# From batch 2 on, key scores in 64x32 tiles with a maximum for each half of the keys, their weights turned by DMA; one more MLP chunk by the seven-product form; a narrower iteration

## The chip, the core and the metric

The kernel runs on one core of a Trainium2 chip. The metric is device microseconds of one execution. A core has a matrix engine (TensorE, "PE" in the profile, with weight loads shown apart as "PEld"), three engines for elementwise work (VectorE "DVE", ScalarE "ACT", GpSimd "POOL"), and SyncE ("SP"), which here issues the DMAs. Data lie in on-chip memory as 128 partitions by columns; matrix products land in eight PSUM banks of 128 x 512 float32.

## The reference, cut

q, k and v have the shape (8 batches, 8 heads, 576 positions, 64); q and k are scaled up by 8.

```python
q_lm = q.reshape(B, H, 32, 18, D).mean(axis=3)      # 32 landmarks
k_lm = k.reshape(B, H, 32, 18, D).mean(axis=3)
A, Bm, C = sm(q, k_lm), sm(q_lm, k_lm), sm(q_lm, k)  # sm: softmax of a b^T / 8
Z = Bm^T / (norm1(Bm) * norminf(Bm) + 1e-6)
for _ in range(6):
    Z = 2 * Z - Z @ Bm @ Z
x = A @ Z @ C @ v                                    # then heads side by side: (8, 576, 512)
u = x + real(fft2(x))                                # over positions and columns
un = layernorm(u)
out = u + relu(un @ w_ch1) @ w_ch2                   # 512 -> 2048 -> 512
```

## The kernel before, in words

**Recording.** The methods of `Kernel` don't emit instructions: they record operations in `Order`, each with a phase, a group, a cost and the tiles it reads and writes. `solve` then lists them by these costs, engine by engine, and takes buffers from pools (`SLOTS`, `BANKS`) as it goes; matmuls between `together` and `apart` stay in one piece. Everything is emitted from one line, L1204 in the profile (L1307 after the change), so groups are told apart by the names of tiles. `SEVEN, LATE = 5, 2`.

**Attention, batch by batch** (`attention`, `landmarks`, `mix`). Heads go in two groups g of four. `lm` holds landmark sums; `qbd` is the landmark queries in blocks, with zeros between. In `landmarks`:
- Bm's scores, softmax, `nrm` (Bm and its row sums), the norms `ci`;
- C's scores for each g: four float32 matmuls `qbd` x `kv` into two banks of 288 keys, one maximum `cb` over both, exp, the sum's reciprocal `cr`;
- `Ce` (C, 128 x 576) turned on PE with the identity (four blocks of 128 and one of 64 into `at` banks, copied to `ml` tiles by ACT), and 20 float32 matmuls for C·v. The result, times `cr` and `ci`, goes into columns 32:96 of the tile `RE`, whose columns 0:32 hold E = 1 − Bm·Z in the block form;
- six rounds of `RE[:, 0:32]` x `RE`, 96 columns wide (the last 64), which square E and carry C·v along; then `pst` and `Wx`, which `mix` takes.

`mix` applies A and the transform over positions, `norm` the layer norm, and it turns `un` by DMA, as two fp16 halves (`hl`), into `unT`.

**MLP**, in 18 chunks of 256 tokens, eight steps i of 256 hidden columns each. Every product of float32 matrices is three fp16 products (high x high, high x low, low x high). The first layer is 48 matmuls of 256 columns per step (`hp<-unT,w`). The second layer of chunks 0 to 4 (`chunk`) is 12 matmuls of 512 columns per step (`acc<-w,h`, or `h` in a `sum` tile). From chunk 5 (`SEVEN`) on, `seven` does it with seven products of quarter matrices, 21 matmuls of 256 columns per step, with sums of weight blocks: three per step (`sums_of`) lie in DRAM and are fetched for each step (`big<-sums`), two (`differences_of`) replace the weights in place. For `seven`, DVE, ACT and POOL make seven combinations of h per step (tiles `ws`, `sum`, `h`). MLP work is low in priority and fills PE where attention waits. E in the code stands for either DVE or POOL.

Attention's products all land in the four `at` banks; `seven` holds two of these from its first chunk on.

Of the kernel before, what the change touches and what calls it, by code (L numbers as in the profile page):

```python
# [98 lines left out]
class Pool:  # L99
    def __init__(self, slots, in_order, kept=False):  # L100
        self.slots, self.in_order, self.kept = slots, in_order, kept
        self.free = list(range(len(slots)))
        self.given, self.made = 0, 0
# [64 lines left out]
class Op:  # L168
    __slots__ = ("engine", "calls", "held", "took", "phase", "group", "margin", "seq", "before", "after", "tiles", "claims", "rank", "start", "end", "nbytes", "port", "name", "other")


class Order:
# [21 lines left out]
    def op(self, engine, held, took, writes, reads, call, nbytes=0, port=False):  # L194
        o = self.bundle if engine == "PE" and self.bundle else None
        if o is None:
            o = Op()
            o.engine, o.calls, o.held, o.took, o.seq = engine, [], 0.0, 0.0, len(self.ops)
            o.phase, o.group, o.margin, o.nbytes, o.port = self.phase, self.group, self.margin, nbytes, port
            o.other = {}  # L200
# [33 lines left out]
    def solve(self):  # L234
# [38 lines left out]

        def able(e, o):
# [8 lines left out]
        while events:  # L283
# [13 lines left out]
            best, again = {}, []  # L297
            for e in engines:
                if free[e] <= now + 1e-9 and ready[e]:
                    best[e] = min((x for x in ready[e] if able(e, x[1]) and fits(x[1])), default=None, key=lambda x: x[0])  # L300
# [5 lines left out]
            for e in [e for e in best if e not in again] + again:  # L306
                found = best[e]
                if found is None or found not in ready[e] or not (able(e, found[1]) and fits(found[1])):
                    found = min((x for x in ready[e] if able(e, x[1]) and fits(x[1])), default=None, key=lambda x: x[0])
# [88 lines left out]
class Kernel:  # L398
    def __init__(self, ctx, tc, NB, q, k, v, w1, w2, t1, t1t, t2, diag, mask, out):
# [13 lines left out]
        for n, (cols, count) in SLOTS.items():  # L413
            self.pools[n] = Pool([self.pool.tile([P, cols], F32, name=f"{n}{i}") for i in range(count)], n in IN_ORDER)
        for n, count in BANKS.items():
            n = "hp" if n == "h" else n
            self.pools[n] = Pool([self.ps.tile([P, 512], F32, name=f"{n}{i}") for i in range(count)], n in IN_ORDER)
# [52 lines left out]
    def turn(self, out, src):  # L470
        self.order.op("SP", 1.22, 1.25, [out], [src], (self.nc.sync, "dma_start_transpose", (out, src), {}))
# [21 lines left out]
    def mm(self, out, a, b, start=True, stop=True, share=1.0):  # L493
# [3 lines left out]
        else:  # L497
            held = max(0.2, 0.02 + 4 * n / 2400) * (m / 128 if m < 128 else 1.0)
# [123 lines left out]
    def load_v(self, b, loads):  # L622
        for g in range(2):
            vf = self.big()
            self.dma(vf.rearrange("p (c d) -> p c d", c=5), self.v[b, g].rearrange("(c p) d -> p c d", p=P))
            loads[g].append(vf)

    def attention(self, b):
# [87 lines left out]
        for u in range(3):  # L716
# [13 lines left out]
            for x in range(0, 8 if u < 2 else 2, 4):  # L730
                n = min(4, AT.shape[1])
                self.turn(AT[:, x : x + n], hl[:, P * x : P * x + P * n])
# [37 lines left out]

    def landmarks(self, b, loads, qbd, lm):
        mm, tr = self.mm, self.tr
        V, A = self.V, self.A
        small = self.small
        flat = lambda t: t.rearrange("p a b -> p (a b)")
        Bd = small([P, 2, 32], "Bd")
        RE = small([P, 2, 96], "RE", bufs=3)
        Ces, crs = [], []

        ps = self.at()  # L780
        self.together()
        for g in range(2):
            for pr in range(2):
                mm(ps[64 * pr : 64 * pr + 64, 32 * g : 32 * g + 32], qbd[:, 2 * g + pr], lm[:, g, 64 + 32 * pr : 96 + 32 * pr])
        self.apart()
        V.tensor_scalar(Bd.rearrange("p g m -> p (g m)"), ps[:, 0:64], 1.0 / 2592.0, None, ALU.mult)
        mx = small(2, "bmx")
        V.tensor_reduce(mx, Bd, AX.X, ALU.max)
        V.tensor_tensor(Bd, Bd, mx.unsqueeze(2).broadcast_to([P, 2, 32]), ALU.subtract)
        A.activation(Bd, Bd, AF.Exp)  # L790
        bs = small(2, "bs")
        V.tensor_reduce(bs, Bd, AX.X, ALU.add)
        V.tensor_scalar(bs, bs, 1e-9, None, ALU.add)
        V.reciprocal(bs, bs)
        nrm = small([P, 2, 2, 32], "nrm", bufs=1)
        V.tensor_tensor(nrm[:, :, 0, :], Bd, bs.unsqueeze(2).broadcast_to([P, 2, 32]), ALU.mult)
        rs = small(2, "rs")
        V.tensor_reduce(rs, nrm[:, :, 0, :], AX.X, ALU.add)
        V.tensor_tensor(
            nrm[:, :, 1, :], self.diag32.unsqueeze(1).broadcast_to([P, 2, 32]),  # L800
            rs.unsqueeze(2).broadcast_to([P, 2, 32]), ALU.mult,
        )

        for g in range(2):
# [24 lines left out]
            Ces.append(Ce)  # L829
            crs.append(cr)  # L830

        psn = self.at()
        mm(psn[:, 0:128], flat(self.ones_bd), nrm.rearrange("p g x m -> p (g x m)"))
# [9 lines left out]
        nbd = self.mid(512).rearrange("p (g i m) -> p g i m", g=2, i=4)  # L843
        for g in range(2):
            self.E.tensor_tensor(
                nbd[:, g].rearrange("p i (d m) -> p i d m", d=2), nrm[:, g, 0].unsqueeze(1).unsqueeze(1).broadcast_to([P, 4, 2, 32]),
                self.mask4.unsqueeze(2).unsqueeze(3).broadcast_to([P, 4, 2, 32]), ALU.mult,
            )
        BT = small([P, 2, 32], "BT", bufs=1)
        for g in range(2):  # L850
            V.transpose(BT[:, g], nrm[:, g, 0, :])
# [7 lines left out]
        for g in range(2):  # L859
            V.scalar_tensor_tensor(RE[:, g, 0:32], pse[:, 32 * g : 32 * g + 32], nci[:, g : g + 1], self.diag32, ALU.mult, ALU.add)  # L860
        ETs = []
        for g in range(2):
            ET = self.mid().rearrange("p (t m) -> p t m", t=5)
            ps = self.at()
            self.order.claim(ET)
            self.together()
            for t in range(4):
                tr(ps[:, 128 * t : 128 * t + 128], Ces[g][:, 128 * t : 128 * t + 128], self.ident)
            self.apart()
            A.copy(ET[:, 0:4].rearrange("p t m -> p (t m)"), ps)  # L870
            ps = self.at()
            self.order.claim(ET)
            tr(ps[:64, 0:128], Ces[g][:, 512:576], self.ident)
            A.copy(ET[:64, 4], ps[:64, 0:128])
            vf = loads[g][2].rearrange("p (c d) -> p c d", c=5)
            ps = self.at()
            self.together()
            for t in range(5):
                n = P if t < 4 else 64
                for i in range(4):  # L880
                    mm(ps[32 * i : 32 * i + 32, 0:64], ET[:n, t, 32 * i : 32 * i + 32], vf[:n, t, 64 * i : 64 * i + 64], t == 0, t == 4)
            self.apart()
            V.tensor_scalar(RE[:, g, 32:96], ps[:, 0:64], crs[g], ci[:, g : g + 1], ALU.mult, ALU.mult)

        for it in range(6):
# [7 lines left out]
            pv = ps[:, 0:192].rearrange("p (g m) -> p g m", g=2)  # L893
            nRE = small([P, 2, 96], "RE", bufs=3)
            if it < 5:
                A.copy(nRE[:, :, 0:32], pv[:, :, 0:32])
            V.tensor_tensor(nRE[:, :, 32:96], RE[:, :, 32:96], pv[:, :, 32:96], ALU.add)
            RE = nRE

        pst = self.at()  # L900
        self.together()
        for g in range(2):
            mm(pst[64 * g : 64 * g + 64, 0:128], RE[:, g, 32:], nbd[:, g, :, 0:32])
# [7 lines left out]
        total = self.order.ops[count]  # L911
        ps = self.at()
        self.together()
        for g in range(2):
            for i in range(4):
                at = 64 * (2 * g + i % 2)
                w = RE[:, g, 32:].rearrange("p (m o) -> p o m", o=2)
# [90 lines left out]
    def norm(self, b, uts):  # L1008
# [23 lines left out]
        for j, ut in enumerate(uts):  # L1032
# [11 lines left out]
            for y in range(2):  # L1044
                self.turn(unT[:, y, :, at : at + P], hl[:, y])
# [39 lines left out]
    def block(self, a, b, op, out=None, sign=1.0):  # L1085

        t = self.new("ws")
        self.E.tensor_tensor(t.rearrange("p (y d) -> p y d", y=2), a, b, op)
        x = t[:, 0:256]
        self.E.tensor_tensor(x, x, t[:, 256:512], ALU.add)  # L1090
        if sign != 1.0:
            self.A.activation(x, x, AF.Copy, scale=sign)
        hl = t[:, 256:512].bitcast(F16).rearrange("p (y d) -> p y d", y=2) if out is None else out
        self.A.copy(hl[:, 0], x)
        self.E.tensor_tensor(hl[:, 1], x, hl[:, 0], ALU.subtract)
        if out is None:
# [6 lines left out]
    def sums_of(self, i):  # L1103
        self.set(1000, -1)
        (b11, b12), (b21, b22) = self.halves(i)
        self.block(b11, b22, ALU.add)
        self.block(b11, b12, ALU.add)
        self.block(b21, b22, ALU.add, sign=-1.0)

    def differences_of(self, i):  # L1110
        self.set(1000, -1)
        (b11, b12), (b21, b22) = self.halves(i)
        self.block(b12, b22, ALU.subtract, b12)
        self.block(b21, b11, ALU.subtract, b21)
# [157 lines left out]
```

## Time and profile before

| | us |
|---|---|
| median of 3 runs | 982.02 (981.95 to 982.12) |
| the profiled execution, whole | 983.1 |
| its span, first to last instruction | 981.3 |
| PE busy in it | 927.6 (95%) |
| DVE / ACT / POOL busy | 761.3 / 467.3 / 202.7 |

The profile is of one execution; 1.8 us of it lie around the span, and it took 1.1 us more than the median. Its page gives busy times and groups of instructions; the trace behind it is asked for windows, waits and timelines. In a timeline PE's instructions overlap: a row's time runs from its first start to its last end, so the room that a piece takes is read from start to start.

### The profile page before, as it was taken

Reading aid. Unit: us, or ns where it says so; the run is one execution under the profiler, and the core shown is the slowest. Engines: PE = TensorE matmul, PEld = TensorE weight load, DVE = VectorE, ACT = ScalarE, POOL = GpSimd, SP = SyncE. Lnnn points to the kernel's source line nnn. Section 1 sums busy time; section 2 is a strip of 40 time slices with the busy share of each in tenths; the row PEclk is TensorE's granted clock in tenths of the full one; section 3 lists DMA queues with packets and bytes.
Section 4 is the critical chain, followed back from the end, with each engine's and each line's share of the span. In section 5 each row is a group of like instructions: output and inputs, shape, how many; then the busy total and the mean of one; then the engine's idle time right before and its main releaser. Section 6 shows DMA issues by size and latency. Waiting matters only on the chain.

```text
span 981.3 us, 25574 instructions
## 1 busy us (share of the span) xinstructions
PE 927.6 (95%) x10354; PEld 735.3 (75%) x10354; DVE 761.3 (78%) x2003; ACT 467.3 (48%) x973; POOL 202.7 (21%) x231
## 2 busy tenths in 40 slices
PE   4666999999999999999999999999999999999997
PEld 2445657566677667888788888888888888888886
DVE  6988986798788789687977898779776677575455
ACT  5999942254434355434543545444634343333332
POOL 0311110224320236111321130212142202011010
PEclk9587999999999999999999999999999999999999
DMA  9885010432423312355524633344332433334231
GB/s 338 265 343 181 4 20 28 141 115 72 152 88 98 123 32 74 94 132 164 159 69 118 191 93 120 106 151 143 108 109 74 125 85 101 97 108 130 82 103 49
DMA packets 139142, 117.32 MB, mean 120 GB/s; under 512 B 66448, under 2 KB 127888, under 8 KB 138896
## 3 DMA queue, kind: packets, MB, share of 16 engines
q1 hardware_dynamic: 139024, 115.69, 39.3%
q8 instruction: 81, 1.33, 0.5%
q14 instruction: 37, 0.30, 0.1%
HBM read 88.91 MB, written 12.58 MB: 103 GB/s over the span
## 4 chain that ended last, share of the span: by engine, by line
PE 83%; DVE 8%; ACT 6%; issue 1%; DMA 1%; SPq 0%; POOL 0%; DVEq 0%; ACTq 0%
PE hp L1204 36%; PE at L1204 24%; PE acc L1204 23%; ACT w L1204 2%; DVE u L1204 2%; ACT ws L1204 1%; ACT big L1204 1%; ACT row L1204 1%; DVE row L1204 1%; DVE sum L1204 1%; ACT ml L1204 1%; ACT h L1204 1%; DMA big<-q_dram 1%; DVE w L1204 1%; DVE h L1204 1%
## 5 line engine op out<-in xcount | busy, mean ns | idle before, releaser
L1204 PE MATMUL hp<-unT,w 128*128 128x256 f16 x3264 | 387.0, 274 | 10.0 <-DMA unT<-row 8.0
L1204 PEld LDWEIGHTS <-w 128*128 128x128 f16 (+1 forms) x3584 | 344.3, 99 | 61.8 <-DMA unT<-row 8.3
L1204 PEld LDWEIGHTS <-h 128*128 128x128 f16 x2508 | 238.8, 98 | 67.5 <-issue 7.0
L1204 PE MATMUL acc<-w,h 128*128 128x256 f16 (+1 forms) x1260 | 204.4, 300 | 0.5 <-DVE u L1204 0.3
L1204 DVE TENSOR_TENSOR sum<-ws 128x256 f32<-128x256 f32 (+1 forms) x266 | 97.9, 416 | 82.0 <-ACT ws L1204 80.9
L1204 ACT ACTIVATE ws<-hp 128x512 f32<-128x512 f32 x104 | 62.0, 596 | 157.7 <-PE hp L1204 157.3
L1204 ACT CAST h<-sum 128x640 f16<-128x640 f32 x104 | 75.3, 724 | 66.9 <-DVE sum L1204 54.8
L1204 PE MATMUL at<-big,h 128*128 128x256 f16 x624 | 102.2, 273 | 0.0
L1204 DVE TENSOR_TENSOR h<-sum,h 128x640 f16<-128x640 f32 x81 | 66.9, 826 | 21.7 <-ACT h L1204 21.0
L1204 POOL TENSOR_TENSOR sum<-ws 128x256 f32<-128x256 f32 (+1 forms) x46 | 32.0, 712 | 234.0 <-ACT ws L1204 189.4
L1204 DVE TENSOR_REDUCE lm<-big 128x32 f32<-128x576 f32 (+1 forms) x48 | 43.9, 942 | 9.8 <-DMA big<-k_dram 8.7
L1204 PE MATMUL at<-w,h 128*128 128x256 f16 x312 | 51.1, 273 | 0.0
L1204 PE MATMUL acc<-big,h 128*128 128x256 f16 x312 | 51.1, 273 | 0.0
L1204 PEld LDWEIGHTS <-big 128*128 128x128 f16 (+1 forms) x768 | 40.0, 104 | 10.8 <-issue 4.3
L1204 POOL TENSOR_TENSOR h<-sum,h 128x640 f16<-128x640 f32 x23 | 32.5, 1412 | 71.5 <-ACT h L1204 70.1
L1204 ACT CAST h<-ws 128x256 f16<-128x256 f32 x104 | 42.1, 404 | 2.6
L1204 DVE SCALAR_TENSOR_TENSOR u<-at,scw,row 128x128 f32<-128x128 f32 (+3 forms) x120 | 39.4, 386 | 3.6 <-PE at L1204 3.3
L1204 DVE TENSOR_TENSOR h<-ws,h 128x256 f16<-128x256 f32 x94 | 40.7, 433 | 0.0
L1204 PEld LDWEIGHTS <-mt 64*128 64x128 f16 (+1 forms) x752 | 28.6, 98 | 15.3 <-issue 9.7
L1204 DVE SCALAR_TENSOR_TENSOR u<-acc,winv,u 128x512 f32<-128x512 f32 x49 | 34.6, 744 | 5.9 <-PE acc L1204 5.7
L1204 ACT ACTIVATE big<-big 128x1168 f16<-128x1168 f32 (+1 forms) x26 | 25.2, 981 | 22.0 <-DMA big<-q_dram 14.8
L1204 POOL TENSOR_TENSOR r<-ve,mhalf 128x2 f32<-128x2 f32 (+1 forms) x20 | 18.0, 899 | 82.5 <-DVE ve L1204 78.0
(193 smaller groups left out, 1310.5 us busy)
## 6 DMA issues: line engine op xcount, KB each, us to landing
big<-sums SPq DMA_DIRECT2D x312, 128.0 KB, 2.1
w<-w_dram SPq DMA_DIRECT2D x22, 512.0 KB, 7.9
big<-v_dram SPq DMA_DIRECT2D x16, 640.0 KB, 4.5
big<-q_dram SPq DMA_DIRECT2D x16, 584.0 KB, 6.6
big<-k_dram SPq DMA_DIRECT2D x16, 576.0 KB, 5.6
out_dram<-u SPq DMA_DIRECT2D x36, 256.0 KB, 2.2
big<-w_dram SPq DMA_DIRECT2D x10, 512.0 KB, 7.2
sums<-ws SPq DMA_DIRECT2D x24, 128.0 KB, 1.8
```

Of the source, the lines that this page charges most:

```text
L1204: getattr(engine, name)(*map(real, args), **{k: real(x) for k, x in kw.items()})
```

## The change

Six things change.

1. `SEVEN` is 4: chunk 4 goes by `seven` as well. The block sums come from `blocks_of`: high and low weights are added once, five blocks per step are made and stored in DRAM, and `differences_of` fetches two of them into place.
2. The iteration works on `ES`, 64 wide (E and S; S starts as Bm, in `nrm`), and C·v stays apart in `R`, multiplied once at the end. `nbd`, the block form, is made from S at the end. The last round is 32 wide.
3. From batch 2 on `keys_turned` replaces `keys` (the old code): `lm` itself is the weight, in tiles of 64 rows by 32 columns. The keys are handled in two halves hf of 288 for each half x of the positions, each with its own maximum and exp; a factor `f` corrects them when both are known. The first half hf takes its 288 columns for x = 1 in two pieces (64 and 224), since the position order wraps. Then weights are split into fp16 high and low, and one DMA turns 18 blocks of 128 (`T`).
4. `values_turned` adds high and low (one add of 640 and one of 512 columns) and makes C·v in 20 float32 matmuls per g; two at the start and two at the end use half of the rows. The PE transposes are gone.
5. The other DMA turns (`AT`, `unT`) go as one of eight blocks, not two of four. v is loaded in three pieces from batch 2 on.
6. `solve` keeps buffers of `at` and `row` for an earlier operation that lacks one (`starved`, `first`), one operation is exempt (`urgent`), `u` tiles are given in order, and costs of turns and of float32 matmuls in small tiles are others.

```diff
-IN_ORDER = ("big", "ml", "mt", "unT", "h", "ws", "sum", "hp", "acc")
+IN_ORDER = ("u", "big", "ml", "mt", "unT", "h", "ws", "sum", "hp", "acc")
+KEEP = ("at", "row")
-SEVEN, RING, LATE, PORT, SPARE = 5, 10, 2, 0.05, 0.1
+SEVEN, RING, LATE, PORT, SPARE = 4, 10, 2, 0.05, 0.1
...
-        self.order.op("SP", 1.22, 1.25, [out], [src], (self.nc.sync, "dma_start_transpose", (out, src), {}))
+        blocks = math.prod(src.shape[1:]) / P
+        self.order.op("SP", 1.15 + 0.016 * blocks, 1.25, [out], [src], (self.nc.sync, "dma_start_transpose", (out, src), {}))
...
+    def keys_turned(self, loads, lm):
...
+        for hf in range(2):
+            banks = [self.at(), self.at()]
+            self.order.claim(Ce)
+            self.together()
+            for g in range(2):
+                for r in range(2):
+                    rows = slice(64 * g + 32 * r, 64 * g + 32 * r + 32)
+                    for x, at, t, n in ((0, 0, 0, 288), (1, 0, 512, 64), (1, 64, 0, 224)) if hf == 0 else ((0, 0, 288, 288), (1, 0, 224, 288)):
+                        half = slice(64 * x, 64 * x + 64)
+                        mm(banks[x][rows, at : at + n], lm[half, g, 32 * r : 32 * r + 32], kv[g][half, r, t : t + n], share=0.5)
+            self.apart()
+            for x in range(2):
+                V.tensor_reduce(cmx[:, x, hf : hf + 1], banks[x][:, 0:288], AX.X, ALU.max)
...
+        for x in range(2):
+            for hf in range(2):
+                c = Ce[:, S * x + 288 * hf : S * x + 288 * hf + 288]
+                A.activation(c, c, AF.Copy, scale=f[:, x, hf : hf + 1])
+            cols = slice(S * x, S * x + S)
+            A.copy(hl[:, 0, cols], Ce[:, cols])
+            self.E.tensor_tensor(hl[:, 1, cols], Ce[:, cols], hl[:, 0, cols], ALU.subtract)
+        T = self.big()[:, 0 : 2 * S].bitcast(F16)
+        self.turn(T.rearrange("p (c m) -> p c m", m=P), hl.rearrange("p y t -> p (y t)"))
...
+    def values_turned(self, loads, T, ci, R):
+        V, mm = self.V, self.mm
+        ET = self.big()[:, 0 : 2 * S]
+        for a, b in ((0, 640), (640, 2 * S)):
+            self.E.tensor_tensor(ET[:, a:b], T[:, a:b], T[:, 2 * S + a : 2 * S + b], ALU.add)
...
+            tiles = [(0, low, 4, 4)] + [(x, slice(0, P), 5 * x + c, c) for c in range(4) for x in range(2)] + [(1, high, 4, 4)]
...
-                    mm(ps[i, 96 * g + c0 : 96 * g + 96], RE[i, g, 0:32], RE[i, g, c0:])
+                    mm(ps[i, 64 * g + c0 : 64 * g + 64], ES[i, g, 0:32], ES[i, g, c0:])
...
-            for y in range(2):
-                self.turn(unT[:, y, :, at : at + P], hl[:, y])
+            self.turn(unT[:, :, :, at : at + P].rearrange("p y c t -> p (y c) t"), hl.rearrange("p y d -> p (y d)"))
...
-        self.block(b12, b22, ALU.subtract, b12)
-        self.block(b21, b11, ALU.subtract, b21)
+        for j, w in enumerate((b12, b21)):
+            self.dma(w, self.sums[5 * i + 3 + j].bitcast(F16).rearrange("p (y d) -> p y d", y=2))
```

Where the instructions stand, first on PE at the key scores of batch 2 (`big_64` and `big_68` or `big_66` hold keys, `at_...` are banks). Before, one g:

```order
L1204 MATMUL hp_107<-big_66,w_110 128x256
L1204 MATMUL at_103<-big_64,qbd_126 64x288 x2
L1204 MATMUL at_102<-big_64,qbd_126 64x288 x2
L1204 LDWEIGHTS h_94
L1204 MATMUL acc_108<-w_111,h_94 128x512
```

And now the first half hf of the first g, of what is one piece for both g:

```order
L1307 MATMUL hp_107<-big_69,w_110 128x256
L1307 MATMUL at_102<-big_68,lm_123 32x288
L1307 MATMUL at_104<-big_68,lm_123 32x64
L1307 MATMUL at_104<-big_68,lm_123 32x224
L1307 MATMUL at_102<-big_68,lm_123 32x288
L1307 MATMUL at_104<-big_68,lm_123 32x64
L1307 MATMUL at_104<-big_68,lm_123 32x224
```

Twelve such matmuls and then eight of 288 columns for the second hf stand where two pieces of four stood; MLP matmuls stand on both sides as before.

On PE at C·v, one g of batch 2 before (`ml_72`, `ml_73`: C and its turned copy):

```order
L1204 MATMUL hp_106<-big_66,w_110 128x256
L1204 MATMUL at_105<-ident,ml_72 128x128 x4
L1204 MATMUL at_104<-ident,ml_72 64x128
L1204 MATMUL at_103<-big_68,ml_73 32x64 x20
L1204 LDWEIGHTS w_110
```

And now, both g of batch 2 (`big_67` is the sum of the turned halves):

```order
L1307 MATMUL hp_106<-big_69,w_110 128x256
L1307 MATMUL at_105<-ES_165 32x64 x8
L1307 MATMUL at_103<-big_64,big_67 32x64 x20
L1307 MATMUL at_104<-big_65,big_67 32x64 x20
L1307 LDWEIGHTS sum_100
```

The two products stand together, behind the first round of the iteration, and no turn by PE is ahead of them.

On DVE at the same place of batch 6, before, where `RE` takes C·v out of its bank:

```order
L1204 TENSOR_TENSOR h_94<-ws_99,h_94 128x256
L1204 TENSOR_TENSOR h_94<-sum_101,h_94 128x640
L1204 TENSOR_REDUCE amx_172<-at_103 128x16
L1204 TENSOR_TENSOR mt_75<-at_103,amx_172 128x512
L1204 TENSOR_SCALAR RE_139<-at_102,cr_155,ci_159 128x64
```

And now, with both subtractions of the low halves (`big_67<-big_64,big_67`) and, behind the DMA turn of `big_67` into `big_65`, the adds (`big_63<-big_65`):

```order
L1307 TENSOR_TENSOR big_67<-big_64,big_67 128x576
L1307 TENSOR_TENSOR sum_101<-ws_97 128x256 x2
L1307 TENSOR_TENSOR sum_101<-ws_97 128x128
L1307 TENSOR_TENSOR h_96<-ws_97,h_96 128x256
L1307 TENSOR_TENSOR big_67<-big_64,big_67 128x576
L1307 TENSOR_TENSOR h_96<-sum_101,h_96 128x640
L1307 TENSOR_TENSOR mt_74<-mt_77,mt_74 128x512
L1307 TENSOR_TENSOR big_63<-big_65 128x640
L1307 TENSOR_TENSOR big_63<-big_65 128x512
```

Two DVE instructions, of 640 and 512 columns, now stand between the last subtraction and the first add.

## Rows read from the trace of the kernel before

**Rows 1.** The page: busy time of each engine, and the chain that ended last.

```profile
PE 927.6 (95%) x10354; PEld 735.3 (75%) x10354; DVE 761.3 (78%) x2003; ACT 467.3 (48%) x973; POOL 202.7 (21%) x231
...
PE 83%; DVE 8%; ACT 6%; issue 1%; DMA 1%; SPq 0%; POOL 0%; DVEq 0%; ACTq 0%
```

**Rows 2.** Windows: start:end, length; busy PE PEld DVE ACT POOL; clock, DMA share, GB/s.

```profile
0.00:100.00 100.00, 60.31 (x760) 44.85 (x761) 83.86 (x227) 83.21 (x169) 18.38 (x25) 0.78 0.81 277
...
350.00:400.00 50.00, 49.42 (x631) 37.59 (x630) 48.76 (x140) 26.62 (x64) 21.96 (x26) 1.00 0.26 73
400.00:962.00 562.00, 558.76 (x6182) 478.09 (x6181) 413.60 (x1067) 241.04 (x479) 102.36 (x113) 1.00 0.40 115
```

**Rows 3.** PE's waits, 100 to 975 us: total us, times, longest.

```profile
PE at L1204 <- DVE u L1204: 3.7, 5, 1.1
...
PE acc L1204 <- DVE u L1204: 0.3, 1, 0.3
```

**Rows 4.** Timeline of PE at key scores: start us, us, instruction.

```profile
590.23 0.49 PE L1204 MATMUL at<-w,h 128*128 128x256 f16 x3
590.65 1.19 PE L1204 MATMUL at<-big,qbd 128*64 128x288 f32 x8
591.77 0.50 PE L1204 MATMUL at<-big,h 128*128 128x256 f16 x3
```

**Rows 5.** Timeline of PE at the turn of C and at C·v.

```profile
605.78 0.71 PE L1204 MATMUL at<-ident,ml 128*128 128x128 f32 x5
606.33 1.15 PE L1204 MATMUL acc<-w,h 128*128 128x256 f16 x9
...
611.18 0.49 PE L1204 MATMUL acc<-w,h 128*128 128x256 f16 x3
611.60 0.90 PE L1204 MATMUL at<-big,ml 128*32 128x64 f32 x40
612.43 0.76 PE L1204 MATMUL at<-kbd,big 128*128 128x64 f16 x20
```

**Rows 6.** Timeline of PE in the iteration, and at 32-wide tiles.

```profile
319.94 1.47 PE L1204 MATMUL acc<-w,h 128*128 128x512 f16 x6
321.34 0.53 PE L1204 MATMUL at<-RE 32*32 32x96 f32 x16
321.81 4.06 PE L1204 MATMUL acc<-w,h 128*128 128x512 f16 x18
...
326.26 4.10 PE L1204 MATMUL hp<-unT,w 128*128 128x256 f16 x36
330.29 0.42 PE L1204 MATMUL at<-RE 32*32 32x64 f32 x16
330.65 0.61 PE L1204 MATMUL hp<-unT,w 128*128 128x256 f16 x4
...
586.87 0.33 PE L1204 MATMUL at<-BT 32*32 32x32 f32 x16
587.12 0.50 PE L1204 MATMUL acc<-w,h 128*128 128x256 f16 x3
```

**Rows 7.** Timeline of PE at 64x32 tiles of fp16, and the records' own durations (ns min/median/max).

```profile
541.50 0.53 PE L1204 MATMUL at<-t,Wt 64*32 64x262 f16 x24
541.97 1.26 PE L1204 MATMUL hp<-unT,w 128*128 128x256 f16 x10
...
L1204 PE MATMUL at<-t,Wt x384: 269/272/423, 43.4 to 761.4; 64*32 64x262 f16 x192
L1204 PE MATMUL at<-big,qbd x128: 406/406/742, 9.7 to 700.4; 128*64 128x288 f32 x128
```

**Rows 8.** DMA turns, of four blocks and of two: issues, us to landing.

```profile
unT<-row SPq DMA_TRANSPOSE x68, 2.5
...
AT<-hl SPq DMA_TRANSPOSE x8, 2.3
```

**Rows 9.** DVE groups by shape: busy us, mean ns, idle before.

```profile
L1204 DVE TENSOR_TENSOR h<-sum,h 128x640 f16<-128x640 f32 x81 | 66.9, 826 | 21.7 <-ACT h L1204 21.0
...
L1204 DVE TENSOR_TENSOR mt<-mt,mt 128x512 f16<-128x512 f32 x11 | 8.0, 730 | 1.9 <-ACT mt L1204 1.8
```

More of the change, by code (lines that the diff above doesn't have):

```diff
@@ L168 @@
 class Op:
-    __slots__ = ("engine", "calls", "held", "took", "phase", "group", "margin", "seq", "before", "after", "tiles", "claims", "rank", "start", "end", "nbytes", "port", "name", "other")
+    __slots__ = ("engine", "calls", "held", "took", "phase", "group", "margin", "seq", "before", "after", "tiles", "claims", "rank", "start", "end", "nbytes", "port", "name", "other", "urgent")
 class Order:
@@ L272, in fits, with starved, first @@
             return True
+        def starved():
+            kept = {}
+            for e in engines:
+                for key, o in ready[e]:
+                    if e != o.engine:
+                        continue
+                    new = [t.pool for t in makes(o)]
+                    for p in new:
+                        if p.name in KEEP and len(p.free) < new.count(p) and (p not in kept or key < kept[p]):
+                            kept[p] = key
+            return kept
+        def first(e):
+            best = None
+            for x in ready[e]:
+                if (best is None or x[0] < best[0]) and able(e, x[1]) and fits(x[1]):
+                    if not x[1].urgent and any(t.pool in kept and x[0][0] > kept[t.pool][0] for t in makes(x[1])):
+                        continue
+                    best = x
+            return best
         def able(e, o):
@@ L296, in solve @@
                                 t.pool.free.append(t.slot)
-            best, again = {}, []
+            best, again, kept = {}, [], starved()
             for e in engines:
                 if free[e] <= now + 1e-9 and ready[e]:
-                    best[e] = min((x for x in ready[e] if able(e, x[1]) and fits(x[1])), default=None, key=lambda x: x[0])
+                    best[e] = first(e)
             both = [best.get(e) for e in ("DVE", "POOL")]
@@ L308, in solve @@
                 if found is None or found not in ready[e] or not (able(e, found[1]) and fits(found[1])):
-                    found = min((x for x in ready[e] if able(e, x[1]) and fits(x[1])), default=None, key=lambda x: x[0])
+                    found = first(e)
                 if found is None or any(
@@ L729, in attention @@
                 self.E.tensor_tensor(hy[:, :, 1], av, hy[:, :, 0], ALU.subtract)
-            for x in range(0, 8 if u < 2 else 2, 4):
-                n = min(4, AT.shape[1])
-                self.turn(AT[:, x : x + n], hl[:, P * x : P * x + P * n])
+            self.turn(AT, hl)
             ATs.append(AT)
@@ L769, in attention, with keys @@
         self.mix(b, ATs, CS, *land())
[L771 to L802, printed above, removed]
+    def keys(self, loads, qbd, lm):
+        V, A, mm, small = self.V, self.A, self.mm, self.small
+        Cs = []
         for g in range(2):
@@ new lines, in values_turned @@
+    def values_turned(self, loads, T, ci, R):
[3 more added lines that the diff above has]
+            self.E.tensor_tensor(ET[:, a:b], T[:, a:b], T[:, 2 * S + a : 2 * S + b], ALU.add)
+        E = ET.rearrange("p (c m) -> p c m", m=P)
+        low, high = slice(0, 64), slice(64, P)
+        for g in range(2):
+            vf = loads[g][2].rearrange("p (c d) -> p c d", c=5)
+            ps = self.at()
+            self.together()
+            tiles = [(0, low, 4, 4)] + [(x, slice(0, P), 5 * x + c, c) for c in range(4) for x in range(2)] + [(1, high, 4, 4)]
+            for x, rows, blk, c in tiles:
+                for r in range(2):
+                    i, at = 2 * r + x, 64 * g + 32 * r
+                    mm(ps[32 * i : 32 * i + 32, 0:64], E[rows, blk, at : at + 32], vf[rows, c, 64 * i : 64 * i + 64],
+                       (x, c) in ((0, 4), (1, 0)), (x, c) in ((0, 3), (1, 4)))
+            self.apart()
+            V.tensor_scalar(R[:, g], ps[:, 0:64], ci[:, g : g + 1], 2.0**-14, ALU.mult, ALU.mult)
@@ L842, in landmarks @@
         V.tensor_scalar(nci, ci, -1.0, None, ALU.mult)
[L843 to L848, printed above, removed]
         BT = small([P, 2, 32], "BT", bufs=1)
         for g in range(2):
-            V.transpose(BT[:, g], nrm[:, g, 0, :])
+            V.transpose(BT[:, g], nrm[:, g, 1, :])
         blocks = [slice(32 * i, 32 * i + 32) for i in range(4)]
@@ L859, in landmarks @@
         for g in range(2):
[L860 to L883, printed above, removed]
+            V.scalar_tensor_tensor(nrm[:, g, 0, :], pse[:, 32 * g : 32 * g + 32], nci[:, g : g + 1], self.diag32, ALU.mult, ALU.add)
+        (self.values if b < LATE else self.values_turned)(loads, Cs, ci, R)
+        ES = nrm[:, :, 0:2].rearrange("p g x m -> p g (x m)")
         for it in range(6):
@@ L1083, in halves, with blocks_of @@
         return [[self.w2s[2 * i + x][:, :, 256 * d : 256 * d + 256] for d in range(2)] for x in range(2)]
[L1085 to L1096, printed above, removed]
+    def blocks_of(self, i):
+        self.set(1000, -1)
+        F = []
+        for x in range(2):
+            F.append(self.new("ws"))
+            w = self.w2s[2 * i + x]
+            self.E.tensor_tensor(F[x], w[:, 0], w[:, 1], ALU.add)
+        (b11, b12), (b21, b22) = [[f[:, 0:256], f[:, 256:512]] for f in F]
+        for a, b, op, sign in (
+            (b11, b22, ALU.add, 1), (b11, b12, ALU.add, 1), (b21, b22, ALU.add, -1), (b12, b22, ALU.subtract, 1), (b21, b11, ALU.subtract, 1)
+        ):
+            t = self.row(512)
+            x = t[:, 0:256]
+            self.E.tensor_tensor(x, a, b, op)
+            if sign < 0:
+                self.A.activation(x, x, AF.Copy, scale=-1.0)
+            hl = t[:, 256:512].bitcast(F16).rearrange("p (y d) -> p y d", y=2)
+            self.A.copy(hl[:, 0], x)
+            self.E.tensor_tensor(hl[:, 1], x, hl[:, 0], ALU.subtract)
             m = self.dram.tile([P, 256], F32, name=f"sums{len(self.sums)}")
```

137 lines of the change are left out of this document (111 added, 26 removed).

## The prediction

> **What bounds the kernel now.** I read the page's busy times and its chain first, then busy times by stretch, then PE's waits, then PE's timeline at each place that the diff touches. PE is busy for 927.6 of 981.3 us and makes 83% of the chain that ends last [rows 1]. Two stages differ. In the first 100 us PE is busy for 60, ACT for 83, DVE for 84, and DMA has a share of 0.81 [rows 2]: the start is bound by loads and by elementwise work, and PE work saved there buys little. From then on PE is the bound: 558.76 of 562 us busy from 400 to 962 at full clock [rows 2], and its waits from 100 to 975 us are four groups, the largest 3.7 us and the smallest 0.3 [rows 3], so at most 14.8 us by these two. So for batches 1 to 7 I cost the change by PE's room. A matmul's row overlaps the next one, so I take room from start to start: from the start of the row ahead to the start of the row behind, less the ahead row's matmuls. The prices of these: from 6 and 18 matmuls of 512 columns in 1.47 and 4.06 us, (4.06 − 1.47)/12 = 0.216 each; from 4 and 36 of 256 columns in 0.61 and 4.10 us, (4.10 − 0.61)/32 = 0.109 each [rows 6].
>
> **The change, part by part.**
>
> *Key scores, batches 2 to 7.* A piece before takes 591.77 − 590.23 − 3 x 0.109 = 1.21 us [rows 4]; two per batch, twelve leave: −14.5. How a piece is made up: eight 64x32 tiles of fp16, 24 matmuls of 262 columns, take 0.47 us by their starts [rows 7], and about 0.09 more for the change of tile shape ahead of them (the 96-wide round has such a gap: 321.34 − 319.94 − 6 x 0.216 = 0.10 [rows 6]). Three rounds at 0.109 x 262/256 are 0.33, so 0.23 is fixed. A float32 matmul is recorded as two passes: eight records for four matmuls [rows 4]. A pass of 288 columns takes 0.406 us in its record where an fp16 one of 262 takes 0.272 [rows 7]; without the 0.11 of columns in the latter, the pass streams for 0.406 − 0.16 = 0.24. The piece before is then 4 x 0.24 + 0.23 = 1.2, as measured: its two tiles run beside each other. After it, the second half hf (eight tiles, two passes each) would be 2 x 0.24 + 0.23 = 0.71. In the first half the pieces of 64 and 224 columns share a tile; equal work, but the second waits for the first, and I take 1.0. That is 1.7 per batch and 10.3 in all: **−4.2**. Bounds: both at 0.71 give −6.0, no gain at all 0, and one pass after another the rival below.
>
> *Turn of C on PE.* Five transposes are 606.33 − 605.78 = 0.55 us [rows 5]; twelve go: **−6.6**.
>
> *C·v.* Before 612.43 − 611.18 − 3 x 0.109 = 0.92 us [rows 5]. After, still five matmuls per column group, but those of half the rows come first and last, in another tile shape: about one more round of two 64-column passes (0.24 x 64/288 x 2 = 0.11) and one more change of shape (0.09) per g, so 12 x 0.2 = **+2.4**; bounds 0 and +4.
>
> *Iteration.* A 96-wide round takes 321.81 − 319.94 − 6 x 0.216 = 0.57, a 64-wide one 330.65 − 326.26 − 36 x 0.109 = 0.47, and 16 records of 32 columns 0.25 by their starts, some 0.35 with the change of shape [rows 6]. Five rounds go from 0.57 to 0.47 and the last from 0.47 to 0.35: 0.62 per batch, and seven batches count (batch 0 lies in the start): **−4.4**. The chain of each round through DVE and ACT keeps its steps, with MLP matmuls in between, as in [rows 6].
>
> *Chunk 4.* 96 matmuls of 512 columns become 168 of 256: 96 x 0.216 − 168 x 0.109 = 20.7 − 18.3 = **−2.4**. The first layer doesn't change.
>
> *The DMA turn of C and what waits for it.* This is the new wait. Nothing in the trace turns 18 blocks: two land in 2.3 us, four in 2.5 [rows 8]. By that slope 18 land in 3.9; in proportion to four, in 11.3. I take 4.5, near the slope, since the nearest rows grow so little. The Trainium skill, page "DMA: Bandwidth & Descriptors", section "Latency and other measured facts", gives a DMA transpose 261 GB/s; by this the 590 KB of 18 blocks stream in about 2.3 us, and behind a start of 2 us the landing would be 4.3 (an estimate) and the sum 0.2 lower per batch at most; no run yet shows it. The adds wait for the landing on DVE or POOL. In DVE's order of batch 6 two instructions stand between, of 640 and 512 columns; such take 0.83 and 0.73 us [rows 9], 1.6 in all. In the other five batches I count 3 to 4 us of such work. So DVE stands for some 3 us in batch 6, and about 1 in the others, 6 to 8 in all; behind the adds on DVE are the h combinations that MLP's second layer takes. DVE has room, 413.6 busy of 562 [rows 2], so PE feels only part: **+2**, bounds 0 and +8. SP issues the turn among fetches of block sums. Since the other turns become one where they were two (the 68 of `unT` [rows 8] among them), SP has less to issue on the whole, and I cost it at nothing; if it were late, the price would be the same wait, per us, as above.
>
> *DVE, ACT, POOL.* The blocks cost 24 fewer adds of 512 columns, the two-step maximum and `cr` go; added are the 12 adds of T, 12 subtractions, and one chunk's h combinations. DVE comes out about equal. ACT gains 20 to 30 us (four scalings and two casts per batch) on 467 [rows 1], which its idle half hides; without that cover it would be most of those 20 to 30 us. The tight stretch is 350 to 400 us, with DVE at 48.76 of 50 [rows 2]: there PE still was busy for 49.42, and this is where an extra chunk by `seven` falls. *The start* (order of loads, kept buffers): ±3, taken as 0, since it is bound by loads and elementwise work that stay.
>
> Sum: −4.2 − 6.6 + 2.4 − 4.4 − 2.4 + 2 = −13.2. Against the profiled execution, 983.1 − 13.2 = 969.9; that run was 1.1 above the median, so the median comes to 982.0 − 13.2 = **968.8 us**.
>
> **The rivals.**
>
> *A: small float32 tiles don't run beside each other* (slower). If each pass waits for the one before it on its tile, in program order, then high and low pass of a matmul stand one behind the other and only neighbours overlap: about 9 passes x 0.24 + 0.23 = 2.4 us for each half, so 12 x 2.4 = 28.8 against 14.5 before, +14.3 in place of −4.2: 987 us. The point at which it decides is 1.9 us per half: there the scores cost 8.8 us more than before and eat all the rest. Against it: the piece before would then take 5 x 0.24 + 0.23 = 1.4 and not 1.21 [rows 4]; C·v, 40 passes on four tiles, would take at least 20 x 0.053 + 0.23 = 1.3 and not 0.92 [rows 5]. For it: no float32 piece on eight tiles is in the trace. The Trainium skill states this rule, page "TensorE: Matmul & The Clock Gate", Part 3, "The mechanism": matmuls start and end in program order, without reordering. By that rule the time is the one just given; the two rows speak for passes that overlap more than it allows. Chance 0.07.
>
> *B: the turn's wait reaches PE in full.* With 6 to 8 us of DVE standing passed on, and a start that is 3 worse, 973 to 979. For it: the largest waits of [rows 3] are on DVE. Chance 0.14, still faster. If the turn lands in proportion, 11.3 us, DVE stands for some 7 us more in each of six batches, and little of that is hidden: near 1005. Chance 0.03.
>
> *C: what PE saves comes back as idle time*, with DVE the bound from 200 to 400 us, where the block sums are made earlier and one more chunk needs combinations: some 13 us of waits, 982. For it: DVE 48.76 of 50 in one stretch [rows 2]; against it: PE's 49.42 of 50 in that same stretch, and no net DVE work is added. Chance 0.06.
>
> *D: PE's room is saved but the planner places pieces worse* (kept buffers hold back MLP work that filled PE): a few us over 100 to 975, at worst the end of B. In the changed order MLP matmuls stand on both sides of each new piece, so it has no chance of its own.
>
> **How the numbers follow.** The forecast has 0.70. Its own range: low end with scores −6.0, C·v 0, no wait and the start 2 better, 982.0 − 19.4 − 2 = about 961; high end with scores 0, C·v +4, wait +8 is 982.0 − 1.4 = 980.6, but all three together are unlikely; I take 963 to 976. To hold 8 in 10 with B: **961.5 to 978**. This kernel's runs tell about 0.2% (2 us) from no change. Faster by more: 0.70 + 0.14 + 0.01 for mixed cases = 0.85; within: 0.05 of C; slower: A 0.07, the long turn 0.03 = 0.10.
>
> **What would show it.** Scores: pieces of 12 matmuls near 1.0 us and of eight near 0.7; over 1.9 each, A. No `ident` turns after batch 1; C·v near 1.1. Iteration rounds of 0.47 and 0.35. The landing of the turn from the DMA view, 4 to 5 us; DVE's or POOL's wait for `big` ahead of the adds, 1 to 3 us, and PE's waits from 100 to 975 us, about 2 us more in all. PE's busy time from 100 us on must fall by some 15 us; if it does and the time doesn't, it was C; if it doesn't fall, A. Wrong I am above all if the 64- and 224-column pieces hold up the six other tiles, or if the start moves by more than 3 us.

## The result: 965.4 us, 16.6 us faster, and the profile after

The changed kernel takes 965.43 us (median of 4, 963.92 to 968.13) against 981.99 before: a ratio of 0.9835, with a 95% interval from 0.9813 to 0.9857. The forecast was 968.8 in a range of 961.5 to 978. The profiled execution took 965.6 us with a span of 963.4; its own runs lie 4 us apart, where those of the kernel before lie 0.4 apart.

Busy times of the page, which answer to [rows 1], and the windows that answer to [rows 2] (the long one ends at 945 us, 18 us ahead of the end as before):

```profile
PE 911.0 (95%) x10510; PEld 731.0 (76%) x10510; DVE 760.1 (79%) x2016; ACT 482.8 (50%) x1007; POOL 216.5 (22%) x250
```

```profile
0.00:100.00 100.00, 65.85 (x803) 50.60 (x804) 87.55 (x235) 86.53 (x176) 13.22 (x20) 0.81 0.84 277
...
350.00:400.00 50.00, 50.00 (x616) 42.83 (x615) 42.26 (x109) 24.13 (x48) 13.98 (x17) 1.00 0.42 119
400.00:945.00 545.00, 538.26 (x6198) 460.02 (x6197) 409.78 (x1080) 246.17 (x495) 111.12 (x122) 1.00 0.43 120
```

The stretch from 200 to 300 us, before and now:

```profile
200.00:300.00 100.00, 99.66 (x1033) 65.91 (x1032) 86.20 (x242) 44.79 (x111) 32.05 (x35) 1.00 0.36 115
```

```profile
200.00:300.00 100.00, 97.27 (x1146) 64.76 (x1145) 91.69 (x249) 53.00 (x136) 45.57 (x59) 1.00 0.49 146
```

PE is busy for 16.6 us less. Idle time was 53.7 us (981.3 − 927.6) and is 52.4, but it has moved: in the first 100 us it fell from 39.7 to 34.1 (busy 60.31 to 65.85), and behind that it rose from 14.0 to 18.3. DVE's total is the same within 1.2 us and ACT has 15.5 more, below the 20 to 30 forecast. The stretch from 350 to 400 us, where DVE had 48.76 of 50, is relaxed; the one from 200 to 300 us is tighter, with DVE at 91.69 of 100 and PE 2.7 us idle (0.3 before).

PE's timeline at the pieces that were costed, in the order first hf of the scores and second hf; then one round of the iteration, C·v of one g, and C·v of both g. They answer to [rows 4 to 6]; a piece's room goes from the start of the row ahead to that of the row behind, less the row ahead.

```profile
399.83 0.93 PE L1307 MATMUL hp<-unT,w 128*128 128x256 f16 x7
400.69 0.74 PE L1307 MATMUL at<-big,lm 64*32 64x288 f32 x24
401.36 0.50 PE L1307 MATMUL acc<-w,h 128*128 128x256 f16 x3
...
405.30 1.47 PE L1307 MATMUL hp<-unT,w 128*128 128x256 f16 x12
406.71 0.72 PE L1307 MATMUL at<-big,lm 64*32 64x288 f32 x16
407.36 1.16 PE L1307 MATMUL acc<-w,h 128*128 128x256 f16 x9
```

```profile
314.71 0.49 PE L1307 MATMUL acc<-w,h 128*128 128x256 f16 x3
315.13 0.43 PE L1307 MATMUL at<-ES 32*32 32x64 f32 x16
315.49 0.50 PE L1307 MATMUL acc<-w,h 128*128 128x256 f16 x3
...
317.63 0.49 PE L1307 MATMUL at<-big,h 128*128 128x256 f16 x3
318.09 1.12 PE L1307 MATMUL at<-big,big 64*32 64x64 f32 x40
319.14 0.50 PE L1307 MATMUL at<-w,h 128*128 128x256 f16 x3
...
431.33 0.49 PE L1307 MATMUL at<-big,h 128*128 128x256 f16 x3
431.75 1.95 PE L1307 MATMUL at<-big,big 64*32 64x64 f32 x80
433.64 1.16 PE L1307 MATMUL acc<-w,h 128*128 128x256 f16 x9
```

The first half of the scores takes 1.53 − 7 x 0.109 = 0.77 us, the second 2.06 − 12 x 0.109 = 0.75: 1.5 per batch where the forecast had 1.7 and before had 2.4. The 64- and 224-column pieces hold up nobody. One g of C·v takes 1.51 − 0.33 = 1.18 (before 0.92); where both g stand together, as in four of the six batches, the pair takes 2.31 − 0.33 = 1.98 (two before, 1.85). A 64-wide round takes 0.78 − 0.33 = 0.45.

The DMA turns, with their landing (us), which answer to [rows 8]; then DVE's wait for the turn of C and PE's largest waits, from 100 to 960 us (total, times, longest), which answer to [rows 3]:

```profile
unT<-row SPq DMA_TRANSPOSE x34, 3.2
...
AT<-hl SPq DMA_TRANSPOSE x8, 2.3
big<-big SPq DMA_TRANSPOSE x6, 4.7
```

```profile
DVE big L1307 <- DMA big<-big: 12.6, 6, 3.5
```

```profile
PE at L1307 <- DVE big L1307: 4.9, 4, 2.7
PE hp L1307 <- DVE h L1307: 2.5, 2, 1.4
PE at L1307 <- DVE nrm L1307: 1.3, 1, 1.3
```

Eighteen blocks land in 4.7 us (4.5 was forecast). DVE stands 12.6 us for them, twice what I had counted, and "DVE big" is now PE's largest wait.

### The profile page after: what moved, and what is told of

Same layout as the page of the kernel before. It is cut to its first block, busy times and chain, and to the rows that moved or that the text cites. A ratio compares the mean times of both kernels' runs of the same rounds, so it can differ in the third digit from the quotient of the medians.

```text
span 963.4 us, 26055 instructions
## 1 busy us (share of the span) xinstructions
PE 911.0 (95%) x10510; PEld 731.0 (76%) x10510; DVE 760.1 (79%) x2016; ACT 482.8 (50%) x1007; POOL 216.5 (22%) x250
## 5 line engine op out<-in xcount | busy, mean ns | idle before, releaser
L1307 PEld LDWEIGHTS <-h 128*128 128x128 f16 x2604 | 247.2, 98 | 61.9 <-issue 6.6
L1307 PE MATMUL acc<-w,h 128*128 128x256 f16 (+1 forms) x1260 | 198.6, 294 | 1.1 <-DVE u L1307 0.4
L1307 ACT ACTIVATE ws<-hp 128x512 f32<-128x512 f32 x112 | 66.6, 595 | 140.1 <-PE hp L1307 139.9
L1307 ACT CAST h<-sum 128x640 f16<-128x640 f32 x112 | 81.1, 724 | 82.6 <-DVE sum L1307 68.1
L1307 PE MATMUL at<-big,h 128*128 128x256 f16 x672 | 110.1, 273 | 0.0
L1307 POOL TENSOR_TENSOR sum<-ws 128x256 f32<-128x256 f32 (+1 forms) x58 | 41.3, 727 | 252.9 <-ACT ws L1307 197.9
L1307 POOL TENSOR_TENSOR h<-sum,h 128x640 f16<-128x640 f32 x33 | 46.4, 1405 | 150.3 <-ACT h L1307 150.3
L1307 ACT CAST row<-row 128x256 f16<-128x256 f32 (+1 forms) x76 | 36.7, 505 | 40.4 <-DVE row L1307 32.2
L1307 PE MATMUL at<-w,h 128*128 128x256 f16 x336 | 55.0, 273 | 0.0
L1307 PE MATMUL acc<-big,h 128*128 128x256 f16 x336 | 55.0, 273 | 0.0
```

The costliest lines, as they stand in the source:

```text
L1307: getattr(engine, name)(*map(real, args), **{k: real(x) for k, x in kw.items()})
```

## The experiments

The kernels were timed in several sets, each with the kernel before beside them, and the changed kernel in the first of them alone. Its median there is 965.3; the kernel before is at 981.8 to 982.9 in them, and a ratio is against it. Each kernel below is the changed one with the edit shown, and "+" and "−" are against the changed one. All medians are of 4 runs (of 5 for the old keys).

**The mark.** 

> The changed kernel once more, as the mark for the kernels beside it: 965.4 us, within 964 to 968.

Measured 965.31 (963.24 to 968.56), ratio 0.9825 [0.9796, 0.9854].

**The wait for the turn of C, alone.** The order of every engine is the one of the changed kernel, word for word; only the DMA and what the adds read differ, so C·v of batches 2 to 7 is left out.

```diff
         self.turn(T.rearrange("p (c m) -> p c m", m=P), hl.rearrange("p y t -> p (y t)"))
+        self.order.ops[-1].calls = []
...
+            w = [self.whole[0][:, j].bitcast(F16)[:, 0 : b - a] for j in range(2)]
+            swap = lambda calls: [(e, n, (x[0], *w, *x[3:]), kw) for e, n, x, kw in calls]
...
```

> The changed kernel with every instruction in the same place, but the six DMA turns of C left out, and the adds behind them read weights instead (so C*v of batches 2 to 7 isn't computed). It measures the wait for the turn by itself. By the forecast's term +2 (bounds 0 and +8) the time falls to 963.4; by the trace of the changed kernel, where DVE waits 12.6 us for these turns and PE 4.9 us for tiles called big from DVE, to about 960.5. Rival (the wait is hidden): 965.4.

Measured 958.98 (958.54 to 961.22), ratio 0.9774 [0.9757, 0.9790]: −6.4. PE's waits from 100 us on (same view as above):

```profile
PE hp L1313 <- DVE h L1313: 2.5, 2, 1.4
PE at L1313 <- DVE nrm L1313: 1.3, 1, 1.3
PE at L1313 <- DVE ES L1313: 0.8, 1, 0.8
...
```

"DVE big" is gone and the next waits stay where they were. PE's idle time behind 100 us falls from 18.3 to 11.3 us. So the term that I put at +2 is +6.4, half of DVE's 12.6 us; by the ratios, 0.9774 against 0.9825 and 0.9835 for the changed kernel, it is 5 to 6. Each turn's time on SP's queue (2.4 to 3.5 us) goes as well; in the order of the run after next, turn and queue time together are worth 2 us at most.

**The same wait, told to the order's rules.** `turn` assumed 2.5 us to landing for four and eight blocks and 2.7 for eighteen; the traces show 2.5 (the kernel before), 3.2 and 4.7. The edit tells the rules of all turns, not of C's alone.

```diff
-        self.order.op("SP", 1.15 + 0.016 * blocks, 1.25, [out], [src], ...
+        self.order.op("SP", 1.15 + 0.016 * blocks, max(1.25, 1.25 + 0.145 * (blocks - 4)), [out], [src], ...
```

> The changed kernel, with the cost of a DMA turn in the order's rules set to what the trace shows (2.5 us to landing for four blocks, 3.2 for eight, 4.7 for eighteen; the rules had 2.5, 2.5 and 2.7), so that other work is placed ahead of the adds. Theory (the turn's wait costs 6.4 us because the order doesn't know of it): 959 to 962. Rival (any new placement moves the time by some 7 us, as LINK did): anywhere from 960 to 973, with the waits for the turn gone but others in their place.

Measured 955.85 (955.62 to 961.33), ratio 0.9746 [0.9719, 0.9773]: −9.5, and the fastest full kernel of all. DVE's wait for the turn, and PE's waits from 100 to 950 us, all there are:

```profile
DVE big L1307 <- DMA big<-big: 2.8, 2, 2.0
```

```profile
PE at L1307 <- DVE qbd L1307: 1.7, 1, 1.7
PE at L1307 <- DVE R L1307: 0.6, 1, 0.6
PE at L1307 <- ACT big L1307: 0.3, 1, 0.3
PE at L1307 <- DVE big L1307: 0.2, 1, 0.2
```

In the changed kernel the first add of all six batches is on DVE; here it is on POOL in two of them, and DVE waits in two.

**What is left of the wait there**, by the same two edits as before, again in an unchanged order. 

> The order with the measured landings, every instruction in the same place, but the six DMA turns of C left out and the adds reading weights (so C*v of batches 2 to 7 isn't computed): the wait that is left there. Theory (the known landing hides the wait): within 2 us of the 955.9 of that order. Rival (that order won its 9.5 us by placement elsewhere, and the wait is still paid): 6 us faster, near 950.

Measured 955.87 (953.51 to 957.60), ratio 0.9725 [0.9705, 0.9745], beside 955.85 and 0.9746 with the turns. The medians are the same and the ratios differ by 2 us, with intervals that overlap, so of the wait 2 us at most are left: the landing, told truly, is hidden. If the wait was worth as much as above, that accounts for about 6 of the 9.5 us; the rest can be placement, as the next run shows.

**Placement alone.**

```diff
-LINK, PATIENCE = 0.05, 0.0
+LINK, PATIENCE = 0.06, 0.0
```

> The changed kernel with one constant of the order's rules moved, LINK from 0.05 to 0.06: the same instructions, placed a little otherwise. Theory (PE's room decides, placement is worth little): within 2 us of 965.4. Rival (placement alone is worth more than most terms of the sum): 4 us or more away, with PE idle from 100 us on up or down by as much.

Measured 972.68 (971.62 to 974.75), ratio 0.9908 [0.9893, 0.9924]: +7.3, with the same 10510 matmuls and the same elementwise work, of which 21 instructions have gone from DVE to POOL. My theory fell: a constant without meaning for the work moves the time by three times the smallest terms of the sum. Its span is 8 to 10 us longer, of which the idle time beyond 100 us tells 1 to 2; MLP work done by 100 us is less (110 first-layer matmuls begun, 155 and 144 in the two profiles of the changed kernel), and PE's pieces lie otherwise. So in every comparison here that lets the order be made anew (the −9.5 above is one), some 7 us are unsure.

**The order rules of before.** The costs that item 6 of the change names stay changed.

```diff
-KEEP = ("at", "row")
+KEEP = ()
-IN_ORDER = ("u", "big", ...
+IN_ORDER = ("big", ...
-        total.urgent = True
+        total.urgent = False
```

> The changed kernel with the order rules of before: no buffers kept for earlier operations, u tiles given in any order, no exempt operation. The forecast put these rules at 0: within 3 us of 965.4. Rival (without them attention's chain comes late, MLP work runs out and PE stands idle): 980 or more.

Measured 968.09 (966.46 to 969.66), ratio 0.9859 [0.9844, 0.9874]: +2.7, as forecast and within placement.

**The old keys, under the new rules.**

```diff
-        Cs = self.keys(loads, qbd, lm) if b < LATE else self.keys_turned(loads, lm)
+        Cs = self.keys(loads, qbd, lm)
...
-        (self.values if b < LATE else self.values_turned)(loads, Cs, ci, R)
+        self.values(loads, Cs, ci, R)
```

> The changed kernel with the old key scores, PE turns of C and C*v in all eight batches; iteration, chunk 4 and order rules stay changed. Theory (PE's room decides): scores +5.6 and transposes +6.5 come back, C*v -2.6 and the wait for the DMA turn -4 go: +5 to +6, 971 us. Rival (the gain lies elsewhere, in the order rules or the start): within 2 us of the changed kernel.

Measured 985.46 (984.84 to 987.10), ratio 1.0036 [1.0023, 1.0049]: +20, slower than the kernel before. About half is one hole on PE. Its timeline there (the bracket is idle time ahead and what ended it):

```profile
417.18 0.49 PE L1307 MATMUL at<-big,h 128*128 128x256 f16 x3
417.60 0.64 PE L1307 MATMUL at<-Wx,mt 64*128 64x64 f16 x32
422.49 1.09 PE L1307 MATMUL at<-R,row 128*64 128x64 f32 x16 [4.24 <-DVE u L1307]
429.49 2.72 PE L1307 MATMUL hp<-unT,w 128*128 128x256 f16 x12 [5.91 <-DMA unT<-row]
```

```profile
429.00:432.00 3.00, 2.51 (x12) 1.72 (x12) 2.26 (x5) 1.09 (x2) 0.00 (x0) 0.50 0.32 45
```

At 417 us PE finishes the last MLP matmul that it has. The next chunk needs `unT`, which hangs on a batch whose `mix` is not done, and PE stands for 4.2 and 5.9 us; then twelve first-layer matmuls take 2.72 us where they take 1.47 otherwise, and the granted clock from 429 to 432 us is 0.50: behind the hole PE runs at the lower of its two clock levels (1.2 GHz). From 400 to 450 us the granted clock is 0.90 on average. PE's room isn't the whole account: MLP work must be there to fill it, and attention must keep ahead.

**The old keys with the old rules.** Both edits above. 

> Old key scores, PE turns and C*v in all batches, and the order rules of before as well; what stays changed is the iteration, chunk 4, the merged turns and the loads of v. Theory (PE's room, and the 985 us of the old keys alone came from rules that don't fit them): 982 - 4.4 - 2.4, about 975. Rival (the old keys leave PE idle under either rules): 983 or more.

Measured 975.30 (974.91 to 975.92), ratio 0.9933 [0.9918, 0.9948], where 975 was expected. PE's largest wait beyond 100 us is 1.8 us; the hole is not there. So the 985 us belong to the old keys under rules (and their placement) that don't suit them, not to the keys.

**The old iteration.**

```diff
-                    mm(ps[i, 64 * g + c0 : 64 * g + 64], ES[i, g, 0:32], ES[i, g, c0:])
+                    mm(ps[i, 96 * g + c0 : 96 * g + 96], RE[i, g, 0:32], RE[i, g, c0:])
...
```

> The changed kernel with the old iteration, 96 columns wide with C*v carried along. Theory (PE's room): 0.63 us in each of seven batches, +4.4, 969.8 us. Rival (the rounds are a chain through DVE and ACT with MLP work between, so PE's room there is not the point, or C*v ready late now holds up the first round): not +4.4 but 0, or over +7 if the first round waits for the DMA turn.

Measured 1047.36 (1045.55 to 1049.65), ratio 1.0663 [1.0644, 1.0681]: +82, far beyond 4.4. PE's largest waits from 400 us on:

```profile
PE hp L1308 <- DMA unT<-row: 22.7, 3, 9.1
PE at L1308 <- DVE u L1308: 14.0, 15, 2.4
PE at L1308 <- DVE row L1308: 10.7, 10, 1.7
```

These are holes of the kind just seen, three of them at `unT`. In this version the first round carries C·v along, so it waits for the DMA turn, the adds and the product; in the changed kernel only the product at the end does. The trace shows it: from the start of the turn to the product at the end it takes 18 to 25 us in the six batches of the changed kernel, and 42 to 53 here, where all rounds stand behind C·v. For batch 3, the changed kernel's turn and product, then this one's:

```profile
306.01 3.52 SPq L1307 DMA_TRANSPOSE big<-big  x1
329.86 0.74 PE L1307 MATMUL at<-R,row 128*64 128x64 f32 x16
```

```profile
333.95 2.67 SPq L1308 DMA_TRANSPOSE big<-big  x1
386.50 0.74 PE L1308 MATMUL at<-RE,row 128*64 128x64 f32 x16
```

I read from this that the narrow iteration's worth, once C is turned by DMA, is that it frees the rounds from the turn; no run takes the turn away here, and the part that placement has in the 82 us is not separated.

**Chunk 4 by the plain form**, with the rules' landing as in the changed kernel and as measured.

```diff
-SEVEN, RING, LATE, PORT, SPARE = 4, 10, 2, 0.05, 0.1
+SEVEN, RING, LATE, PORT, SPARE = 5, 10, 2, 0.05, 0.1
```

> The changed kernel with chunk 4 by the plain form. Theory (PE's room): 96 matmuls at 0.216 in place of 168 at 0.109, +2.4, 967.8 us. Rival (DVE is crowded from 200 to 300 us by the block sums and the extra combinations): 0 or faster by up to 3 us, with less PE waiting for DVE before 400 us.

Measured 962.57 (962.02 to 963.34), ratio 0.9799 [0.9784, 0.9814]: −2.7 where +2.4 was expected.

> The same with chunk 4 by the plain form. If the 2.7 us that the plain form won before were waits that the known landing also removes, the two forms now differ by PE's room alone: 2.4 us slower than the run beside it. If DVE's crowding is the cause, it is again about 3 us faster. Placement alone may hide either.

Measured 974.71 (972.95 to 977.88), ratio 0.9929 [0.9908, 0.9949]: 18.9 slower than the same rules with chunk 4 by `seven`. The first of the two has this wait of DVE:

```profile
DVE big L1307 <- DMA big<-big: 7.7, 4, 2.4
```

That is 5 us less than in the changed kernel: in two of the six batches the first add is on POOL here, where the changed kernel has all six on DVE. The second has the hole of the old keys, 4.2 us at `u` and 5.9 at `unT`. So neither run tells what the chunk is worth; it stays inconclusive, and DVE's crowding isn't shown.

**The merged turns.**

```diff
-            self.turn(unT[:, :, :, at : at + P].rearrange("p y c t -> p (y c) t"), hl.rearrange("p y d -> p (y d)"))
+            for y in range(2):
+                self.turn(unT[:, y, :, at : at + P], hl[:, y])
...
```

(The turn of A's weights, `AT`, is split in the same way.)

> The changed kernel with the turns of A's weights and of the layer norm's output as two of four blocks again; the turn of C stays one of eighteen. The forecast put the merging at 0: within 3 us of 965.4, but placement may move it by 7. If the merged turns made the start 3 to 4 us shorter, MLP work done by 100 us falls by as much.

Measured 970.91 (970.30 to 972.47), ratio 0.9884 [0.9868, 0.9901]: +5.5. SP's queue at the first `unT` tiles (start, time, count), of the changed kernel, of the kernel before, of this one, and of the run with the moved constant ("Placement alone"):

```profile
71.17 5.34 SPq L1307 DMA_TRANSPOSE unT<-row  x4
```

```profile
71.86 10.78 SPq L1204 DMA_TRANSPOSE unT<-row  x8
```

```profile
71.14 10.91 SPq L1310 DMA_TRANSPOSE unT<-row  x8
```

```profile
74.30 5.93 SPq L1307 DMA_TRANSPOSE unT<-row  x4
```

A turn holds the queue for about 1.3 us whether it moves four blocks or eight, and PE waits for these tiles there (8.9 us in one wait in the changed kernel's profile, 8.0 in two before, 11.3 in two in this one). The first-layer matmuls begun by 100 us (PE busy and count, of this tile alone; a step has 24 of them, not the 48 given with the kernel before: 3264 from `unT` and 192 from `big` over 144 steps), in the same order:

```profile
0.00:100.00 100.00, 19.37 (x155) 0.81 0.84 277
```

```profile
0.00:100.00 100.00, 15.07 (x116) 0.78 0.81 277
```

```profile
0.00:100.00 100.00, 16.24 (x120) 0.76 0.86 276
```

```profile
0.00:100.00 100.00, 15.54 (x110) 0.78 0.86 275
```

The lead at 100 us is 39 matmuls (28 in the other profile of the changed kernel), 3 to 4 us at 0.109, and without the merging it is down to 4. But the run with the moved constant keeps the merged turns and has no lead at all: its first `unT` turn starts 3.1 us later. So the merged turns free some 5.5 us of SP's queue there, and that the start's gain comes from them is likely, but not shown: placement alone takes the same lead away. Nor is the +5.5 told from placement.

## Why the prediction came out right, point by point

| step | forecast | measured, how |
|---|---|---|
| key scores | −4.2 | −5.4: 6 x 1.52 against 12 x 1.21, by the timelines |
| PE turns of C | −6.6 | −6.6: they are gone from batch 2 on |
| C·v | +2.4 | +1.5: 4 x 0.13 where both g stand together, 2 x 0.5 elsewhere |
| iteration | −4.4 | −4.6 by room: 7 x (5 x 0.11 + 0.10), rounds from 0.56 to 0.45 and the last from 0.45 to 0.35; its worth in time is not settled (1047 without it) |
| chunk 4 | −2.4 | −2.4 by count and price; its worth in time not settled |
| wait for the DMA turn | +2 | +6.4, order unchanged (5 to 6 by the ratios) |
| start | 0 | −5.6 of idle time in this profile; −2.1 in that of the run without the turn of C, whose order is the same |
| sum | −13.2 | −16.7 with the first of these, −13.2 with the second; the medians say −16.6 |

- **The bound was read rightly.** PE's busy time fell by 16.6 us; the five PE terms say −17.5 by the measured prices. The time moved by as much because the two steps that I sized wrongly, the wait and the start, nearly cancel: +6.4 − 5.6 against +2. That the two agree to 1 us is luck in part: the same 10510 matmuls keep PE busy for 905.4 us with the measured landings in the rules and for 917.6 with the moved constant.
- **The scores' step was mis-sized by a little.** I gave the first half 1.0 us for its two pieces per tile, and it takes 0.77. (Two slips of the forecast: at 1.9 us per half the scores cost 8.3 us more than before, not 8.8; and 7 x 0.62 is 4.3.) Rival A, passes one behind another, fell clearly: 24 passes on eight tiles in 0.77 us, not 2.4. The rule of the Trainium skill ("TensorE: Matmul & The Clock Gate", Part 3, "The mechanism"), that matmuls start and end in program order, does not describe these float32 pieces. In the records the first 224-column pass starts at 400.83 us, behind a 288-column pass at 400.75 that the program has later.
- **The wait's step failed at its cover, not at its landing.** 4.7 us was 4.5. I took the DVE instructions between subtraction and add as work that hides the landing, and counted 6 to 8 us of standing; it was 12.6, and PE felt half of it, not a third. The bounds of 0 and +8 held it. Rival B was that wait passed on in full; half of it was, and the sum of the other terms, by the table, made up for it.
- **The start's step was mis-sized.** I took the start as 0, and put the merged turns at nothing on SP, because SP had less to issue. It holds 2.1 to 5.6 us less idle time. The merged turns are the likely cause, since SP's queue works on the first `unT` for 5.3 us and not 10.8; as the moved constant takes the lead away with the turns still merged, the cause stays open.
- **Placement (rival D) should have had a chance of its own.** A constant moved by a fifth cost 7.3 us. That my sum met the result to 3.4 us is partly luck; the chain before → old keys with old rules (−6.5; the iteration and the chunk were −6.8) → turned keys with old rules (−7.2; the terms of the keys, as forecast, −6.4) → new rules (−2.7; forecast 0) agrees better than placement lets one claim.
- **Rival C** (saved room comes back as idle time through DVE's crowding) did not happen in that size. From 350 to 400 us DVE had 42.26 of 50 where it had 48.76; from 200 to 300 us, where most block sums are stored, it rose from 86.20 to 91.69 and PE's idle time from 0.3 to 2.7 us, far from the rival's 13.

## What to carry to other kernels

Where one engine is busy for 95% of the span, cost a change by that engine's room, from start to start in the timeline, but look also for what has to be ready to fill the room: a chain that comes late turns saved room into a hole. When the order of a kernel is made from costs, put the landings that the trace shows into it (here −9.5 us for one line, about 6 of them the wait), and move a constant without meaning once, to learn how far placement alone moves the time, before any single undo is believed. To price one wait, keep the order and take away only what is waited for.

## What was unexpected of the hardware

- Float32 matmuls of 64 rows by 32 columns on eight tiles run beside each other almost fully: 24 passes (eight of them pieces of 64 columns, eight of 224) in 0.77 us, where sixteen passes of 288 columns alone take 0.75.
- A DMA turn between on-chip tiles holds the queue for about 1.3 us at four blocks (10.8 us for eight turns) and the same at eight (5.34 for four); at eighteen it holds it for 2.4 to 3.5. To landing it takes 2.5 us at four blocks, 3.2 at eight, 4.7 at eighteen.
- After a hole of 4.2 and 5.9 us PE's first twelve matmuls took 2.72 us in place of 1.47, at a granted clock of 0.50.
